# Loads of k and v in runs of 18 rows, and both modes of a pair in one 128-row product with a zero-padded block

## The chip, the core and the metric

The kernel runs on one core of one Trainium2 chip. A core has five engines that run side by side and wait for each other through semaphores: TensorE (PE, matrix products; PEld is its weight load), VectorE (DVE), ScalarE (ACT), GpSimd (POOL) and SyncE (SP). In this kernel POOL and SP mainly issue transfers, which 16 DMA engines carry out. POOL's transfers form one queue, served in order of issue; it also converts float32 to 16 bits on the way. SP's form another. The metric is the device time of one execution in microseconds (us), lower is better; the time given is the median of several executions.

## The reference

Two layers follow each other. With phi(x) = elu(x) + 1, the first is a linear attention over 8 batches, 8 heads, 576 rows and 64 columns:

```python
kv  = einsum('bhsd,bhse->bhde', phi(k), v)
z   = sum(phi(k), axis=2)
x   = einsum('bhsd,bhde->bhse', phi(q), kv) / (einsum('bhsd,bhd->bhs', phi(q), z) + 1e-6)
```

Its result is reordered to x of 8 x 576 x 512. The second is a spectral mix with a residual and a channel product:

```python
X = rfft(x, axis=1)                       # the first 64 modes are used
Yr[m] = Xr[m] @ w_r[m] - Xi[m] @ w_i[m]   # one 512x512 pair of matrices for each mode
Yi[m] = Xr[m] @ w_i[m] + Xi[m] @ w_r[m]
u = x + irfft(Y, n=576, axis=1)
out = u + relu(u @ w_ch)
```

The inputs are float32: q, k and v of 9.4 MB each, w_r and w_i of 67 MB each. The output is 9.4 MB of float32.

## The kernel before, in words

**Stage A, attention and forward transform.** `load(b)` has POOL fetch q, k and v of batch b (L179 to L194). q arrives in runs of 18 rows of a head (2304 bytes at 16 bits) and two such runs per partition; k and v arrive in runs of 9 rows (1152 bytes) and four per partition, one for each pair of heads. `exps` (ACT) and `features` (DVE) form phi; `features` also copies v into `vp`, beside a column of ones. `turn_q` transposes phi(q). `sum_kv` (L254) forms the products of phi(k) and v, with z as the 65th column: for two head groups and nine rows, two products of 64 partitions each, in the two halves of PE's rows. Two ACT copies bring the sums to `kv_all`. `form_x` divides and makes x. `transform` multiplies x by the Fourier matrix, and `place_x` spreads the result over partitions, into `xt_c` (DVE and ACT copies, L349 and L350). The raw tiles of q, k and v have two buffers each, so batch b + 2 is loaded when b is used up. Within a loop step the order on each engine is that of the program (`pin`).

**Mode products.** The weights come in pairs of modes: a tile `w` holds both modes of a pair, the first in partitions 0 to 63, the second in 64 to 127 (`w_load`, L114, one transfer for w_r and one for w_i, 1 MB each at 16 bits). Pairs 0 to 4 have buffers of their own and are queued during stage A. After them, in the same queue, stand `wch16` and `pick_sb`, a small table of ones and zeros. From pair 5 on there are two buffers, so POOL issues pair p + 2 when the products of p are done. `mode_pair` (L465) multiplies each pair: for 16 slices `dc`, one product of 64 rows for either mode (`product`, L435), into four 32-row strips of a PSUM tile for each mode, 32 products in all. `evacuate` copies the two PSUM tiles out, one on DVE (L452) and one on ACT (L454). `picks` (L457) sums the four strips with `pick_sb`, four products for each mode, into `yt_ps`, which a DVE copy takes out every fourth pair. Between the products and the picks, and after them, `work_slot` runs pieces of other work (attention rows again for the output, the inverse transform, the channel product), shared out over the pairs. `keep_warm` adds filler products in late pairs. The last pair has its own routine, `last_pair` (L488): its weights lie over all 128 partitions, and its last transfers are small pieces.

**Output.** When the last mode is known, 18 pairs of accumulators are finished one after the other: PE adds the rest of the inverse transform (L736) and `e0` (L775), ACT applies the relu, DVE adds x (L809), and SP stores (`store`, L787). One accumulator pair is 512 KB of output. `QUADS` (L802) names batches whose two halves are stored together once both are done, in runs of 8 KB; the others go half by half in runs of 4 KB. The tiles of rows 512 to 575 and the first few tiles go in runs of 2 KB.

Of the kernel before, what the change touches and what calls it, by code (L numbers as in the profile page):

```python
# [10 lines left out]
F32 = mybir.dt.float32  # L11
F16 = mybir.dt.float16
BF16 = mybir.dt.bfloat16
# [3 lines left out]
NJ = 9  # L17
# [3 lines left out]
def _dft_consts(S: int, NM: int):  # L21

    m = np.arange(NM)
    s_cols = np.concatenate([4 * np.arange(128) + jj for jj in range(4)] + [512 + np.arange(NP)])
    s_rows = np.concatenate([s_cols, s_cols[512:]]).reshape(5, 128).T
    ang = 2.0 * np.pi * s_rows[:, :, None] * m / S
    by_parity = np.concatenate([m[0::2], m[1::2]])
    fwd = np.concatenate([np.cos(ang)[:, :, by_parity], -np.sin(ang)[:, :, by_parity]], axis=2)

    scale = np.where(m == 0, 1.0, 2.0) / S  # L30
    ang = 2.0 * np.pi * np.outer(m, np.arange(S)) / S
    inv = np.empty((NM, 2, S), dtype=np.float64)
    inv[:, 0, :] = np.cos(ang) * scale[:, None]
    inv[:, 1, :] = -np.sin(ang) * scale[:, None]
    pick = np.zeros((128, 16), dtype=np.float16)
    for quad in range(4):
        for c in range(16):
            pick[quad * 32 + c, c] = 1.0

    return fwd.astype(np.float16), inv.reshape(2 * NM, S).astype(np.float16), pick  # L40
# [3 lines left out]
def kernel(  # L44
# [10 lines left out]
    nc = tc.nc  # L55

    B, H, S, Dh = q.shape
    D = H * Dh
    NM = moe_w_r.shape[0]
    NHP = H // 2  # L60
    NDC = D // 128
    NJJ = 4
    NDW = 4 * NDC
    NDL = NDW // 2
    NMP = NM // 2
    XDC = 2 * B * NMP
    NL = 8
    NE = NM - NL
    NF = NM // 2
# [10 lines left out]

    id16 = const.tile([128, 128], F16, name="id16")
    fwd_sb = const.tile([128, 5, 2 * NM], F16, name="fwd_sb")
    pick_sb = const.tile([128, 16], F16, name="pick_sb")
    wch16 = const.tile([128, NDC, D], F16, name="wch16")
    actwarm = const.tile([128, 1], F32, name="actwarm")
    nc.vector.memset(actwarm, 0.0)
# [4 lines left out]

    def xt_cols(dc: int, kk: int, n: int):

        if kk // 2 == LAST:
            part, dc = slice(0, 128), (dc // NDC * 2 + kk % 2) * NDC + dc % NDC
        else:
            part = HALVES[kk % 2]
        c0 = dc * XDC + kk // 2
        return xt_c[part, c0 : c0 + (n - 1) * NMP + 1 : NMP]


    QW = 4 * NJ * NP
# [5 lines left out]
    pin = tc.keep_in_program_order  # L108
# [31 lines left out]
    psA = psA_ctx.enter_context(tc.tile_pool(name="psA", bufs=1, space=bass.MemoryType.PSUM))  # L140
    n_pre, n_keep = W_PRE, W_KEEP

    vp = sA.tile([128, NHP, NJ, 66], F16, name="vpad")
    nc.vector.memset(vp[:, :, :, 64:66], 1.0)

    pending = [(p, half) for p in range(n_keep + n_pre) for half in range(2)]
# [31 lines left out]
    def load(b):  # L178
        for nm, src in (("q", q), ("k", k), ("v", v)):  # L179
            rows_in = src[b].rearrange("h s d -> (h s) d").rearrange(  # L180
                "(hp r j) d -> r hp (j d)", r=128, j=2 * NJ if nm == "q" else NJ
            )
            if (nm, b) == ("q", 0):
                for c in range(2):
                    t = sA.tile([128, 2, NJ * Dh], F32, tag="x16", bufs=2, name=f"q32_{c}")
                    pin(nc.sync.dma_start(out=t, in_=rows_in[:, :, c * NJ * Dh : (c + 1) * NJ * Dh]))
                    raw[nm, b, c] = t
                pin(nc.sync.dma_start(out=id16, in_=id16_dr.ap()))
                pin(nc.sync.dma_start(out=fwd_sb, in_=fwd_dr.ap()))
                continue  # L190
            shape = [128, 2, 2 * NJ * Dh] if nm == "q" else [128, NHP, NJ * Dh]
            t = sA.tile(shape, F16, tag=f"{nm}16", bufs=2, name=f"{nm}16_{b}")
            pin(nc.gpsimd.dma_start(out=t, in_=rows_in))
            raw[nm, b] = t  # L194

    def heads(nm, b, c):
        if (nm, b) == ("q", 0):
            return raw[nm, b, c].rearrange("p o (j d) -> p o j d", d=Dh)
        if nm == "q":
            return raw[nm, b].rearrange("p o (c j d) -> p c o j d", c=2, d=Dh)[:, c]  # L200
        return raw[nm, b].rearrange("p (o c) (j d) -> p c o j d", o=2, d=Dh)[:, c]

    def flat(nm, b):
        tiles = [raw[nm, b, c] for c in range(2)] if (nm, b) == ("q", 0) else [raw[nm, b]]
# [48 lines left out]

    def sum_kv(b):  # L254

        kv_ps = psA.tile([128, 2, 512], F32, tag="big", bufs=3, name=f"kvp{b}")
        for hpp in range(2):
            for j in range(NJ):
                for h2 in range(2):
                    pin(  # L260
                        nc.tensor.matmul(
                            kv_ps[:, h2, hpp * 130 : hpp * 130 + 130],
                            phi["k", b][HALVES[h2], hpp, j].rearrange("p o d -> p (o d)"),
                            vp[HALVES[h2], hpp::2, j, 0:65],
                            start=(j == 0),
                            stop=(j == NJ - 1),
                        )
                    )
        for hpo in range(2):
            rows = HALVES[hpo]  # L270
            pin(
                nc.scalar.copy(  # L272
                    out=kv_all[b][rows],
                    in_=kv_ps[rows, :, 0:260].rearrange("p t (c o n) -> p c t o n", c=2, o=2)[
                        :, :, :, hpo, :
                    ],
                )
            )

    def form_x(b, jj):  # L280
        if jj == 0:
# [150 lines left out]
            if work:  # L432
                work.pop(0)()

    def product(P, kk: int, w, dc: int):  # L435
        last = kk // 2 == LAST
        n_dc = NDL if last else NDW
        c = dc % NDC * 32
        n = 32 if dc < NDC else 2 * B
        rows = slice(0, 128) if last else HALVES[kk % 2]  # L440
        pin(
            nc.tensor.matmul(  # L442
                P[c : c + n, :], xt_cols(dc, kk, n), w[rows, dc, :],
                start=(dc < NDC), stop=(dc >= n_dc - NDC), tile_position=(rows.start, c),
                skip_group_check=True,
            )
        )

    def evacuate(kk: int, P):
        st = ystage.tile([128, D], F16, tag="ystage", bufs=2, name=f"ys{kk}")  # L450
        if kk % 2 == 0:
            pin(nc.vector.tensor_copy(out=st, in_=P))  # L452
        else:
            pin(nc.scalar.copy(out=st, in_=P))  # L454
        return st

    def picks(kk: int, st):  # L457
        for ec in range(NDC):
            pin(
                nc.tensor.matmul(  # L460
                    yt_ps[:, ec, kk % 8, :], st[:, ec * 128 : ec * 128 + 128], pick_sb
                )
            )

    def mode_pair(p: int):  # L465
        nonlocal yt_ps
        w = w_get(p)
        kks = (2 * p, 2 * p + 1)
        if p % 4 == 0:
            yt_ps = psW.tile([128, NDC, 8, 2 * B], F32, tag="yt", bufs=1, name=f"yt{p // 4}")  # L470
        Ps = [psW.tile([128, D], F32, tag="P", bufs=2, name=f"P{kk}") for kk in kks]
        for dc in range(NDW):
            for P, kk in zip(Ps, kks):
                product(P, kk, w, dc)
        sts = [evacuate(kk, P) for P, kk in zip(Ps, kks)]
        work_slot(p, "mid")
        for kk, st in zip(kks, sts):
            picks(kk, st)
        if p % 4 == 3:
            if kks[1] < NF:  # L480
                pin(nc.vector.tensor_copy(out=YE_T[:, :, kks[1] - 7 : kks[1] + 1, :], in_=yt_ps))
            else:
                g = (kks[1] - NF) // NL + 1
                pin(nc.vector.tensor_copy(out=YL[:, :, :, g, :], in_=mode_rows(yt_ps)))
        work_slot(p, "end")
        keep_warm(FILL.get(p, 0))

    def last_pair():  # L488
        w = w_get(LAST)
        kk = NM - 2  # L490
        work_slot(LAST, "start")
        P = psW.tile([128, D], F32, tag="P", bufs=2, name=f"P{kk}")
        for dc in range(NDL):
            product(P, kk, w, dc)
        st = evacuate(kk, P)
        work_slot(LAST, "mid")
        picks(kk, st)
        pin(nc.vector.tensor_copy(out=Y8[:, :, 0 : NL - 1, :], in_=yt_ps[:, :, 0 : NL - 1, :]))
        keep_warm(3)
        kk = NM - 1  # L500
        y_last = psW.tile([128, NDC, 2 * B], F32, tag="P", bufs=2, name="y_last")
        for dc in range(NDL):
            for ec in range(NDC):
                pin(
                    nc.tensor.matmul(
                        y_last[:, ec, :], w[:, NDL + dc, ec * 128 : ec * 128 + 128],
                        xt_cols(dc, kk, 2 * B),
                        start=(dc == 0 and ec == 0), stop=(dc == NDL - 1), skip_group_check=True,
                    )
                )  # L510
        nc.vector.tensor_copy(out=Y8[:, :, NL - 1, :], in_=y_last)
# [29 lines left out]

    yt_ps = None

    for p in range(n_early):
        mode_pair(p)
    wpre_ctx.close()
# [252 lines left out]
            in_=x_tail[i // 2],  # L799
        )  # L800

    QUADS = (2, 4, 5, 6)  # L802

    def finish(n: int):
        acc = accs[n]
# [190 lines left out]
```

## Time and profile before

| | us |
|---|---|
| median of 9 runs (lowest to highest) | 425.06 (424.51 to 426.32) |
| the profiled execution | 426.32 |
| its span, first to last instruction | 424.5 |
| PE busy (share of the span) | 278.5 (66%) |
| DVE busy | 215.0 (51%) |
| ACT busy | 161.0 (38%) |
| POOL busy | 56.7 (13%) |
| queue of POOL's transfers | 16512 packets, 81.47 MB |
| queue of SP's transfers | 3680 packets, 11.22 MB |

Mean granted PE clock: 0.788 of full. Busy shares are means over stages that have different limits. The page has six parts: busy time, the span in 40 slices with tenths of busy time and the DMA rate, the queues, the chain of work that ended last, the groups of instructions, and the transfers. A stretch of time in the profile gives a line with its length, the busy time and the number of instructions of PE, PEld, DVE, ACT and POOL, the granted PE clock, the share of the DMA engines' time that packets took (over 1 where they overlap) and the GB/s moved.

### The profile page before, as it was taken

To read this page: it belongs to the slowest core of one execution; us is meant where nothing else is said; L and a number is where in the kernel's file an instruction comes from. 1 tells how busy PE (TensorE), PEld (TensorE's weight loads), DVE (VectorE), ACT (ScalarE), POOL (GpSimd) and SP (SyncE) were. 2 spreads that over 40 slices of the span, in tenths; PEclk is the share of its full clock that TensorE was granted. 3 is DMA by queue.
4 is the path that set the end of the run, shared out by engine and by line. 5 is a ranking of instruction groups with operands and counts; after the bars stand their busy time and mean duration, and the time that the engine had idled before them with its cause. 6 is when DMAs were issued, how large, how long until landed. Compare 5 with 4: busy or idle time off the path is not lost.

```text
span 424.5 us, 7976 instructions
## 1 busy us (share of the span) xinstructions
PE 278.5 (66%) x3426; PEld 149.7 (35%) x3426; DVE 215.0 (51%) x446; ACT 161.0 (38%) x253; POOL 56.7 (13%) x99
## 2 busy tenths in 40 slices
PE   1358377688516644434344777989797698989991
PEld 0246266566302322212122232434343333455320
DVE  4599489895203453355444443445263323413892
ACT  4688487844202102000000243445354341421881
POOL 4222124210000100000000011100000000030000
PEclk9999888989755555555555598889899986998997
DMA  9999999999999999999999999999999999994697
GB/s 214 209 209 215 207 218 203 227 207 218 223 212 220 215 215 213 219 218 215 214 219 216 216 213 219 216 217 213 218 218 217 215 215 218 216 209 97 247 411 283
DMA packets 20227, 93.20 MB, mean 220 GB/s; under 512 B 2016, under 2 KB 11104, under 8 KB 15520
## 3 DMA queue, kind: packets, MB, share of 16 engines
q0 software_dynamic: 16512, 81.47, 93.6%
q1 hardware_dynamic: 3680, 11.22, 7.0%
q8 instruction: 27, 0.44, 0.4%
q14 instruction: 8, 0.07, 0.0%
HBM read 163.93 MB, written 9.44 MB: 408 GB/s over the span
## 4 chain that ended last, share of the span: by engine, by line
DMA 63%; PE 22%; DVE 5%; ACT 4%; issue 3%; POOL 2%; DVEq 0%; POOLq 0%; ACTq 0%
DMA w<-in_moe_w_i_dram 48%; PE P L442 8%; DMA pick_sb<-row_pick 8%; DMA k<-in_k_dram 7%; PE acc L736 3%; PE acc L775 2%; PE zl L425 2%; ACT ke L213 2%; POOL w L119 1%; PE eps L677 1%; ACT qT L249 1%; DVE ys L452 1%; PE z L699 1%; PE yt L460 1%; DVE x L299 1%
## 5 line engine op out<-in xcount | busy, mean ns | idle before, releaser
L442 PE MATMUL P<-w,xt_c 64*32 64x512 bf16 (+2 forms) x1000 | 51.7, 545 | 58.7 <-DMA w<-in_moe_w_i_dram 57.3
L452 DVE CAST ys<-P 128x512 f16<-128x512 f32 x32 | 22.1, 691 | 124.0 <-PE P L442 124.0
L454 ACT CAST ys<-P 128x512 f16<-128x512 f32 x31 | 18.1, 585 | 155.9 <-PE P L442 155.9
L119 POOL DMA_DIRECT2D w<-in_moe_w_r_dram x31 | 17.0, 550 | 245.9 <-PE P L442 96.4
L442 PEld LDWEIGHTS <-xt_c 64*32 64x32 bf16 (+2 forms) x1000 | 16.6, 128 | 79.3 <-DMA w<-in_moe_w_i_dram 46.1
L165 PEld LDWEIGHTS <-qT 64*128 64x128 f16 (+1 forms) x640 | 22.9, 123 | 51.6 <-issue 29.2
L677 PE MATMUL eps<-wch,xTw 128*128 128x512 f16 x144 | 40.8, 411 | 0.0
L165 PE MATMUL num<-kv,qT 64*128 64x65 f16 (+1 forms) x320 | 13.8, 211 | 27.3 <-ACT kv L272 13.8
L658 DVE TENSOR_TENSOR x_main<-ya,x_main 128x512 f32<-128x512 f32 x32 | 21.9, 688 | 15.0 <-PE ya L654 14.9
L660 ACT CAST x16w<-x_main 128x512 f16<-128x512 f32 x32 | 19.8, 618 | 23.5 <-DVE x_main L658 22.4
L165 PE MATMUL nw<-kv,qT 64*128 64x65 f16 (+1 forms) x320 | 19.0, 240 | 9.4 <-DVE x_tail L621 4.3
L685 ACT CAST E<-eps 128x512 f16<-128x512 f32 (+1 forms) x40 | 21.2, 540 | 9.2 <-PE eps L677 9.2
L460 PE MATMUL yt<-pick_sb,ys 128*128 128x16 f16 x252 | 11.7, 174 | 17.8 <-DMA pick_sb<-row_pick 11.2
L299 DVE TENSOR_TENSOR x<-num,rd 128x512 f16<-128x512 f32 x32 | 22.1, 691 | 1.1
L213 ACT ACTIVATE qe<-q 128x1152 f16<-128x1152 f16 (+1 forms) x16 | 17.9, 1157 | 11.0 <-DMA q<-in_q_dram 10.9
L242 PE MATMUL qTp<-id,qe 128*128 128x128 f16 x144 | 14.1, 276 | 10.1 <-DVE qe L226 9.5
L249 ACT COPY qT<-qTp 128x1152 f16<-128x1152 f16 x16 | 19.6, 1296 | 0.4 <-PE qTp L242 0.2
L460 PEld LDWEIGHTS <-ys 128*128 128x128 f16 x252 | 9.7, 102 | 28.4 <-DVE ys L452 15.0
L213 ACT ACTIVATE ke<-k 128x1152 f16<-128x1152 f16 x16 | 17.7, 1152 | 4.9 <-DMA k<-in_k_dram 4.9
L425 PE MATMUL zl<-wch,id 128*128 128x512 f16 x72 | 19.5, 406 | 0.0
L785 ACT ACTIVATE acc<-acc 128x512 f32<-128x512 f32 x34 | 18.1, 582 | 2.4 <-PE acc L736 1.2
L119 POOL DMA_DIRECT2D w<-in_moe_w_i_dram x31 | 16.9, 544 | 4.1 <-DMA q<-in_q_dram 2.3
(113 smaller groups left out, 460.3 us busy)
## 6 DMA issues: line engine op xcount, KB each, us to landing
w<-in_moe_w_r_dram POOLq DMA_DIRECT2D x31, 1024.0 KB, 12.2
w<-in_moe_w_i_dram POOLq DMA_DIRECT2D x31, 1024.0 KB, 16.9
k<-in_k_dram POOLq DMA_DIRECT2D x8, 576.0 KB, 12.8
v<-in_v_dram POOLq DMA_DIRECT2D x8, 576.0 KB, 14.9
out_dram<-x_main SPq DMA_DIRECT2D x4, 1024.0 KB, 4.9
q<-in_q_dram POOLq DMA_DIRECT2D x7, 576.0 KB, 12.9
out_dram<-x_main SPq DMA_DIRECT2D x6, 512.0 KB, 4.6
q<-in_q_dram SPq DMA_DIRECT2D x2, 576.0 KB, 4.5
```

Of the source, the lines that this page charges most:

```text
L119: nc.gpsimd.dma_start(out=w_in[p][half::2], in_=two.rearrange("g (r dc) e -> (g r) dc e", dc=NDW))
L165: mm = nc.tensor.matmul(num[hpo][orow, c0 : c0 + 65], qT[rows, hpp, h2, cols], kv_sb[rows, hpp, h2, :])
L213: pin(nc.scalar.activation(out=ev[:, c], in_=heads(nm, b, c), func=AF.Exp))
L249: nc.scalar.copy(out=qT[:, :, c * NJ : (c + 1) * NJ], in_=qT_ps.rearrange("p j x -> p x j"))
L299: nc.vector.tensor_tensor(out=dst.rearrange("p (o c d) -> p o c d", o=2, c=4), in0=nv[:, :, :, 0:64], in1=rden.unsqueeze(3).broadcast_to([ ...
L425: pin(nc.tensor.matmul(last_ps[0], id16, wch16[:, 0, :]))
L442: nc.tensor.matmul(P[c : c + n, :], xt_cols(dc, kk, n), w[rows, dc, :], start=(dc < NDC), stop=(dc >= n_dc - NDC), tile_position=(rows.sta ...
L452: pin(nc.vector.tensor_copy(out=st, in_=P))
L460: nc.tensor.matmul(yt_ps[:, ec, kk % 8, :], st[:, ec * 128 : ec * 128 + 128], pick_sb)
L658: pin(nc.vector.tensor_tensor(out=x, in0=acc, in1=x, op=ALU.add))
L677: nc.tensor.matmul(e_ps, xT[:, c, :], wch16[:, c, :], start=(c == 0), stop=(c == NDC - 1))
L685: pin(nc.scalar.copy(out=dst, in_=e_ps[:, cols]))
```

## The change

Four edits:

- k and v are loaded in runs of 18 rows like q. A partition then holds rows of two heads, and 32 partitions hold one head of each. So `sum_kv` works in 32-row groups: for each of two pairs of groups, 18 rows and two groups, 72 products for a batch in place of 36. Each pair has its own PSUM tile, and there are four ACT copies of 64x130 in place of two of 64x260.
- In `mode_pair` both modes multiply as one product over 128 partitions. The stationary block `xz` has 32 columns: 16 for the first mode, which are zero in partitions 64 to 127, and 16 for the second, which are zero in partitions 0 to 63. Two such blocks are cleared once; `set_diagonal` fills the next pair's with two DVE copies, ahead of `evacuate`. There are 16 products for a pair in place of 32, one PSUM tile, and one evacuation, on DVE for even and on ACT for odd pairs.
- `picks` handles both modes at once: `pick_sb` has 32 columns, and there are four products for a pair in place of eight.
- `QUADS` holds batches 5 and 6 only; batches 2 and 4 are stored half by half.

The last pair keeps its products.

```diff
-    pick = np.zeros((128, 16), dtype=np.float16)
+    pick = np.zeros((128, 32), dtype=np.float16)
...
-    vp = sA.tile([128, NHP, NJ, 66], F16, name="vpad")
+    vp = sA.tile([128, 2, 2 * NJ, 66], F16, name="vpad")
...
             rows_in = src[b].rearrange("h s d -> (h s) d").rearrange(
-                "(hp r j) d -> r hp (j d)", r=128, j=2 * NJ if nm == "q" else NJ
+                "(hp r j) d -> r hp (j d)", r=128, j=2 * NJ
             )
...
-        kv_ps = psA.tile([128, 2, 512], F32, tag="big", bufs=3, name=f"kvp{b}")
-        for hpp in range(2):
-            for j in range(NJ):
+        for pair in range(2):
+            kv_ps = psA.tile([128, 2, 512], F32, tag="big", bufs=3, name=f"kvp{b}_{pair}")
+            for j in range(2 * NJ):
                 for h2 in range(2):
+                    r0 = 64 * pair + 32 * h2
                     pin(
                         nc.tensor.matmul(
-                            kv_ps[:, h2, hpp * 130 : hpp * 130 + 130],
-                            phi["k", b][HALVES[h2], hpp, j].rearrange("p o d -> p (o d)"),
-                            vp[HALVES[h2], hpp::2, j, 0:65],
+                            kv_ps[:, h2, 0:130],
+                            phi["k", b][r0 : r0 + 32, j // NJ, j % NJ].rearrange("p o d -> p (o d)"),
+                            vp[r0 : r0 + 32, :, j, 0:65],
...
+                            tile_position=(r0, 0),
                         )
                     )
...
+            for hpo in range(2):
+                rows = HALVES[hpo]
+                pin(
+                    nc.scalar.copy(
+                        out=kv_all[b][rows, pair], in_=kv_ps[rows, :, hpo * 65 : hpo * 65 + 65]
+                    )
+                )
...
+    def set_diagonal(p: int):
+        for h in range(2):
+            src = xt_v[HALVES[h], :, :, :, p].rearrange("p c t b -> p c (t b)")
+            pin(nc.vector.tensor_copy(out=xz[p % 2][HALVES[h], :, h, :], in_=src))
...
-        Ps = [psW.tile([128, D], F32, tag="P", bufs=2, name=f"P{kk}") for kk in kks]
+        P = psW.tile([128, D], F32, tag="P", bufs=2, name=f"P{p}")
         for dc in range(NDW):
-            for P, kk in zip(Ps, kks):
-                product(P, kk, w, dc)
-        sts = [evacuate(kk, P) for P, kk in zip(Ps, kks)]
+            product(P, xz[p % 2][:, dc].rearrange("p h n -> p (h n)"), 32, w, dc, NDW)
+        if p + 1 < LAST:
+            set_diagonal(p + 1)
+        st = evacuate(p, P)
         work_slot(p, "mid")
-        for kk, st in zip(kks, sts):
-            picks(kk, st)
+        picks(2 * p, st, 2)
...
+    xz = [ystage.tile([128, NDW, 2, 2 * B], BF16, name=f"xz{i}") for i in range(2)]
+    for i in range(2):
+        nc.vector.memset(xz[i], 0.0)
+    set_diagonal(0)
     for p in range(n_early):
         mode_pair(p)
...
-    QUADS = (2, 4, 5, 6)
+    QUADS = (5, 6)
```

## The prediction

> **What bounds the kernel now.** I read the page's slices first, then its chain, then the transfer queues in short stretches, then the order of instructions at the end.
>
> ```profile
> DMA  9999999999999999999999999999999999994697
> GB/s 214 209 209 215 207 218 203 227 207 218 223 212 220 215 215 213 219 218 215 214 219 216 216 213 219 216 217 213 218 218 217 215 215 218 216 209 97 247 411 283
> ...
> DMA 63%; PE 22%; DVE 5%; ACT 4%; issue 3%; POOL 2%; DVEq 0%; POOLq 0%; ACTq 0%
> DMA w<-in_moe_w_i_dram 48%; PE P L442 8%; DMA pick_sb<-row_pick 8%; DMA k<-in_k_dram 7%; PE acc L736 3%; PE acc L775 2%; PE zl L425 2%; ACT ke L213 2%; POOL w L119 1%; PE eps L677 1%; ACT qT L249 1%; DVE ys L452 1%; PE z L699 1%; PE yt L460 1%; DVE x L299 1%
> ```
>
> The 16 DMA engines are full in 37 of 40 slices. Loads keep them full until about 386 us, then there is a hole of some 7 us around 390, then the stores run. In the chain, matrix products (PE P L442) are 8%; even those lie between landings of w. So up to 386 us the time is bytes over rate: work on PE, DVE and ACT counts there only if it lets the queue run empty. After that, it counts.
>
> The rate isn't the same everywhere. Stretches by time, with GB/s last; in each, the transfer counts tell what is in flight:
>
> ```profile
> 12.20:14.00 1.80, 0.00 (x0) 0.10 (x1) 1.76 (x3) 0.00 (x0) 0.00 (x0) 1.00 1.13 218
> 15.00:20.00 5.00, 2.09 (x36) 1.81 (x35) 2.19 (x3) 3.96 (x4) 1.29 (x2) 1.00 1.21 208
> 51.20:53.00 1.80, 0.52 (x10) 0.46 (x10) 0.06 (x1) 1.20 (x2) 0.00 (x0) 0.50 1.11 212
> 77.00:80.00 3.00, 1.67 (x43) 1.42 (x41) 2.97 (x5) 2.98 (x5) 0.54 (x1) 1.00 1.21 206
> 150.00:340.00 190.00, 122.08 (x1395) 56.12 (x1395) 84.61 (x217) 50.62 (x93) 20.08 (x38) 0.71 1.02 216
> ```
>
> The transfers of the second stretch alone:
>
> ```profile
> DMA packets 920, 1.04 MB, mean 208 GB/s; under 512 B 17, under 2 KB 920, under 8 KB 920
> ```
>
> Every packet is under 2 KB, so it is k and v. At 12.2 to 14 and 51.2 to 53 nearly all are above 2 KB: q. So k and v move at 206 to 209, q at 209 to 218, w at 216.
>
> At the end, stores and their gap (columns as above):
>
> ```profile
> 400.00:402.00 2.00, 2.00 (x14) 0.57 (x12) 2.00 (x3) 1.90 (x4) 0.00 (x0) 1.00 0.99 401
> 402.00:404.00 2.00, 2.00 (x16) 0.57 (x12) 1.92 (x3) 1.68 (x4) 0.00 (x0) 1.00 0.51 209
> 410.00:417.00 7.00, 5.29 (x32) 1.50 (x30) 6.92 (x6) 4.78 (x10) 0.00 (x0) 1.00 1.00 411
> ```
>
> And 402 to 404 in 40 slices of 0.05 us:
>
> ```profile
> DMA  9979959200000000000000000009993009999003
> ```
>
> 19 empty slices, from 402.40 to 403.35: for 0.95 us there is nothing to send, while DVE is at work.
>
> **What the Trainium skill says.** "DMA: Bandwidth & Descriptors", section "Why small descriptors are slow (HBM only)": each packet pays a fixed few cycles and each transfer fixed metadata, so longer runs are faster. The trace agrees in sign (208 against about 213). "Perfetto Trace Analysis", section "DMA Optimizations": runs under 2 KB are costly and batching up to 8 KB can help a lot. Here the help is small: stores in 4 KB runs make 401, in 8 KB runs 411. "TensorE: Matmul & The Clock Gate", section "Part 3: Packing small matmuls — row/col tiling": products in different row or column groups overlap. The trace agrees: 32 products of 64x512 take 1.10 us at full clock, not 32 times 0.2.
>
> **The change part by part.**
>
> *Loads.* 16 loads of 576 KB, 9.44 MB, go from 1152-byte to 2304-byte runs, as q has. 9.44/207.5 is 45.5 us, 9.44/212.5 is 44.4: 1.1 us less; I take 1.0. If q's rate in a short stretch is chance and equals k's, 0; if q reached w's 216, 1.8.
>
> *k-v sums (stage A).* 36 products per batch become 72, still two row groups at once, since a pair's products are all issued before the other's. 36 took 1.22 to 1.45 us, so PE gets 1.2 to 1.5 more; if 32-row products don't overlap, up to 3.7. ACT copies: two of 64x260 at 0.37 become four of 64x130, about 0.30 each by the slope between 256 columns (0.39) and 512 (0.585): 0.45 more. Behind the second pair's copies on ACT stand the next exps; `num` on PE waits for them, and DVE for that; the v copy to `vp` waits for the last product, and v's next load for the copy. I take a slip of 1.2 us a batch, off the path: q of batch 7, the closest load, is issued at 67.84 and lands 9.2 later, of which its own bytes take 2.8 and, as an estimate, 2 are fixed: over 4 us of cover, against one sum between the landing that feeds it (49.5) and it. Pair 5's w is issued at 114.81, after stage A, and its first half lands 15.6 later: less 4.9 and 2, 8.7 us of cover against five sums, 6 us. Also the first picks wait for pick_sb until 125.65 (issued at 92.73, 32.92 to landing, by the chain in order of time) while their input is ready at 115.3. So it costs 0.
>
> *Products.* 32 of 64x512 become 16 of 128x512. The last pair's 8 of that shape take 0.66 us; twice that, less one start, is about 1.1: equal to the 1.10 of 32. At half clock both are four rounds, 1.95. Evacuations halve (0.69 on DVE or 0.58 on ACT, in turn, before on both at once); picks fall from 8 (0.36) to 4 (0.26), twice as wide. Added: two `set_diagonal` copies a pair, 64 partitions by 256 elements. No row has this shape; 128x64 takes 0.20 and an elementwise 128x256 0.42: 0.3 each, bounds 0.2 and 0.45, so 0.6 us of DVE a pair, less 0.35 for the evacuation saved every other pair. They stand ahead of `evacuate` on DVE, and run while PE works or waits on w. DVE is busy 84.61 of 190 us there. Two memsets (0.27) and the first copies delay pair 0 by 1.2 us, under the wait for pick_sb. Without that cover it would be 1.2. Once: pair 30 to the last product is PE without idle, from w's landing at 380.71 to 391.6; its picks and fewer weight loads save 0.2 us there.
>
> *Stores.* b = 2 and b = 4 go in two halves. DVE finishes an accumulator pair every 1.22 us from 397.67; b=2's first half is ready at 401.3 and can flow at 402.4, when DMA falls idle, in place of 403.35. From there to 421.5 DMA is full, so 0.95 us comes off the end, less 2.1 MB at 401 in place of 411 (0.13) and a new gap of about 0.15 before b=5's 1 MB: 0.7. It can't exceed 3.6: the last store (512 KB), issued at 417.05, lands 6.5 later; the 1 MB one that was issued into the empty queue took 4.2, so half of it with nothing ahead would take about 2.9.
>
> *Sum.* On the profiled execution, 426.32 (span 424.5 and 1.8 around it): 1.0 + 0.2 + 0.7 = 1.9 less, 424.4. That run is the slowest of nine; their median is 425.06, so 423.2, 0.45% faster.
>
> **The rivals.**
>
> 1. *The gains are taken back (no change).* The loads' gain is as small as 0.3, because 208 against 213 is read from stretches of 2 us; or the store gap only moves, as a 1 MB store still waits for both halves of b=5. For it: the spread of q's stretches. Against it: all four k-v stretches lie within 206 to 209. One gain missing leaves 0.3 to 0.9 us: 424.5.
>
> 2. *The 32-row products run one after another and the queue runs dry (slower).* Two now share 68 ns; alone, 72 take 4.9 us, 3.7 more a batch. Five such slips, about 17 us after overlap, exceed the 8.7 of cover at pair 5's w: the queue stands empty 8 to 9 us near 126. Net 425.06 + 8.5 - 1.9 = 431.7. It decides from 1.7 us a batch. Against it: today's two groups do overlap.
>
> 3. *DVE becomes late for products (less gain).* If `set_diagonal` took over 1 us and stood behind the folds, PE would wait for it, not for w. Cover: w is issued with 6 us of other transfers ahead. It would need 6 us a pair; it could only show at pair 30, some 0.5 to 1 us: 424.0.
>
> **How the numbers follow.** Both gains, rival 3 with them: 0.64, 422.3 to 424.2, likeliest 423.2. Rival 1: 0.20, 424.2 to 425.9. Rival 2: 0.08; slower by what I don't see: 0.08. The range, 422.3 to 425.8, leaves out the slower cases and a little on either side. A difference under 0.2% (0.85 us) can't be told from none: faster 0.66, same 0.18, slower 0.16.
>
> **What would show it.** Loads right: k-v stretches at 211 to 215 GB/s, and pick_sb landing at about 124.7 in place of 125.65. Stage A right: products of pair 0 before 121, DMA slices still 9 throughout. Products right: L442's successor about 1.1 us a pair at full clock. Stores right: no empty DMA at 402, end 1.5 to 2 us earlier. I am wrong if a slice near 115 to 130 or 140 shows DMA below 9, or if PE is at half clock when the stores begin: a half-rate PE couldn't feed them.

## The result, and the profile after

The changed kernel takes 422.03 us (median of 10 runs, 421.43 to 424.69); the kernel before, run beside it, 425.74 (32 runs). The ratio is 0.9926, 95% interval 0.9913 to 0.994: 0.74% or 3.15 us faster (2.6 to 3.7). The prediction said 1.9 us, 423.2. The direction holds, but the gain is 1.25 us larger, and the time lies 0.3 below the low end of the range (422.3). That margin is thin: timed again (below) the same kernel took 422.35, just inside the range. The record also lists two runs, 422.58 and 424.09, that are not among the ten; with them the median would be 422.33.

The times of either kernel fall into groups 1 to 1.5 us apart (of the changed one, a profiled execution with PE at half clock after the last weights took 423.18, one without it 421.84), so times are compared below by ratios with their intervals, and places in the trace by their own records.

The profiled execution after is 423.18 us (span 421.4), against 426.32 (424.5): 3.14 less. Its slices, its transfers and its chain, the lines that answer to those shown of before:

```profile
PEclk9999998589855555555555598899799896899897
DMA  8999999999999999999999999999999999996797
GB/s 217 211 212 216 210 219 207 225 221 207 222 214 222 220 205 222 219 205 223 219 210 218 219 215 213 219 217 213 220 216 210 221 221 207 221 210 128 245 392 311
DMA packets 16417, 93.17 MB, mean 221 GB/s; under 512 B 2032, under 2 KB 2944, under 8 KB 11968
...
q8 instruction: 24, 0.39, 0.3%
...
DMA 63%; PE 22%; DVE 5%; issue 3%; ACT 3%; POOL 2%; DVEq 0%; ACTq 0%; POOLq 0%
```

DMA stays at 9 from the second slice to the hole near 388: the loads set the time up to there, as before. The hole is shallower (6 and 7 in place of 4 and 6). There are 8160 fewer packets under 2 KB than the 11104 of before. The line to keep in mind is the least conspicuous: queue q8 carries *instructions* (packets, MB, share of the DMA engines' time). Before it read:

```profile
q8 instruction: 27, 0.44, 0.4%
```

Three packets fewer, of 16 KB each. That is 0.05 MB of 93, and, as is shown below, it is where most of the unforeseen gain comes from.

The new groups of instructions (line, engine, operation, tiles; then busy us and mean ns of one; then idle time before them):

```profile
L431 PE MATMUL P<-w,xz 128*32 128x512 bf16 x496 | 47.6, 523 | 64.2 <-DMA w<-in_moe_w_i_dram 61.8
...
L256 PE MATMUL kvp<-vpad,ke 32*128 32x130 f16 x576 | 24.3, 261 | 8.9 <-ACT qT L243 6.1
L441 DVE COPY xz<-xt_c 64x256 bf16<-64x256 bf16 x62 | 23.0, 371 | 11.0 <-PE P L431 10.1
```

Products wait for w as before. `set_diagonal` takes 371 ns a copy (0.3 estimated), the k-v products 24.3 us of PE in all (11.8 before).

Stretches after (length, busy us and number of PE, PEld, DVE, ACT, POOL, then PE clock, DMA share, GB/s). The first three hold k and v, the last two the end of the loads and the first stores:

```profile
15.00:20.00 5.00, 2.05 (x36) 1.77 (x36) 2.19 (x3) 4.06 (x4) 1.16 (x2) 1.00 1.11 213
24.00:28.00 4.00, 1.85 (x38) 1.28 (x38) 3.72 (x15) 2.56 (x5) 1.44 (x2) 1.00 1.11 213
75.00:78.00 3.00, 3.00 (x62) 2.81 (x61) 1.43 (x2) 2.39 (x4) 0.54 (x1) 0.50 1.11 211
384.00:392.00 8.00, 7.57 (x68) 3.79 (x67) 2.52 (x5) 1.12 (x3) 0.45 (x1) 0.80 0.25 45
392.00:400.00 8.00, 8.00 (x42) 3.05 (x40) 6.80 (x8) 6.83 (x13) 0.12 (x1) 0.98 0.88 307
```

And the last two stretches before:

```profile
384.00:392.00 8.00, 7.68 (x84) 3.63 (x80) 1.96 (x4) 0.59 (x1) 0.00 (x0) 0.96 0.42 79
392.00:400.00 8.00, 7.75 (x43) 3.73 (x44) 5.84 (x8) 6.04 (x13) 0.57 (x1) 1.00 0.63 209
```

k and v move at 211 to 213 (206 to 209 before). From 392 to 400 DMA is busy 88% in place of 63%: the stores begin earlier.

Where the 3.14 us come from is seen in the chain of waits in order of time (start, length, what), at its two turns. Before:

```profile
362.95 17.72 DMA w<-in_moe_w_i_dram
380.71 1.55 PE P L442 x24
...
390.71 0.92 PE y_last L505 x32
```

After:

```profile
91.74 33.08 DMA pick_sb<-row_pick
125.13 1.86 PE P L431 x12
...
362.71 25.30 DMA w<-in_moe_w_i_dram x2
388.67 0.47 PE ypl L908 x4
```

`pick_sb` lands at 124.82 (125.65 before). Then, near 362.8, the second half of pair 30's w is issued at nearly the same time in both, and waits in a full queue. Before it took 17.72 us to land; after, the list of transfers issued there has

```profile
w<-in_moe_w_i_dram POOLq DMA_DIRECT2D x1, 1024.0 KB, 15.4
```

which is 2.3 less, though the first of its 16 engines was only 1.0 us earlier (374.42 against 375.43). Second, before, PE was the last at the end: the last piece of w landed at 389.89, but `y_last` was done only at 391.65. After, the last piece lands at 388.02 and `y_last` is done at 388.39, right behind it; the chain runs through transfers there ("x2"), and PE waits for them.

The timeline at that point after (start, duration, engine, instructions, in brackets the idle time before and who ended it):

```profile
388.39 0.22 DVE L508 CAST Y<-y_last 128x64 f16<-128x64 f32 x1 [1.58 <-PE y_last L502]
388.67 0.47 PE L908 MATMUL ypl<-id,Y 128*128 128x128 f16 x4 [0.32 <-DVE Y L508]
...
392.82 2.94 SPq L792 DMA_DIRECT2D out_dram<-x_main  x4
```

From the end of `y_last` to the first store 4.43 us pass, before 3.33 (391.65 to 394.98). The difference is PE's clock: half of full for one stretch of 3.41 us. The kernel before has such a stretch too, but earlier, at the products of pair 30. The two stretches, before and after (columns as above):

```profile
381.22:384.63 3.41, 3.41 (x41) 1.41 (x26) 1.08 (x2) 0.58 (x1) 0.00 (x0) 0.50 1.02 210
388.86:392.27 3.41, 3.38 (x16) 1.84 (x14) 1.15 (x3) 1.12 (x3) 0.57 (x1) 0.50 0.00 0
```

So the difference of the two profiled executions divides like this: last piece of w 1.87 earlier, of which 1.0 is the load stream itself and 0.85 the slowest DMA engine; PE no longer late behind it, 1.4; PE at half clock before the first store, 1.1 back; from the first store's issue to the end 28.6 in place of 29.5, 0.95. Together 1.0 + 0.85 + 1.4 - 1.1 + 0.95 = 3.1. The 1.4 and the 1.1 both go with the half clock (for the first, see the kernel with the instructions put back), so they belong to these two executions as much as to the kernels, and nearly cancel.

### The profile page after: what moved, and what is told of

Same layout as the page of the kernel before. It is cut to its first block, busy times and chain, and to the rows that moved or that the text cites. A ratio compares the mean times of both kernels' runs of the same rounds, so it can differ in the third digit from the quotient of the medians.

```text
span 421.4 us, 7345 instructions
## 1 busy us (share of the span) xinstructions
PE 291.4 (69%) x3094; PEld 157.2 (37%) x3094; DVE 228.1 (54%) x495; ACT 154.0 (37%) x253; POOL 57.0 (14%) x99
## 2 busy tenths in 40 slices
DMA packets 16417, 93.17 MB, mean 221 GB/s; under 512 B 2032, under 2 KB 2944, under 8 KB 11968
## 4 chain that ended last, share of the span: by engine, by line
DMA 63%; PE 22%; DVE 5%; issue 3%; ACT 3%; POOL 2%; DVEq 0%; ACTq 0%; POOLq 0%
DMA w<-in_moe_w_i_dram 51%; DMA pick_sb<-row_pick 8%; PE P L431 7%; DMA k<-in_k_dram 3%; PE acc L737 3%; PE kvp L256 2%; PE acc L776 2%; POOL w L116 2%; DVE x L292 1%; PE eps L678 1%; PE zl L418 1%; ACT ke L207 1%; PE ya L655 1%; PE xTp L668 1%; ACT qT L243 1%
## 5 line engine op out<-in xcount | busy, mean ns | idle before, releaser
L431 PE MATMUL P<-w,xz 128*32 128x512 bf16 x496 | 47.6, 523 | 64.2 <-DMA w<-in_moe_w_i_dram 61.8
L448 ACT CAST ys<-P 128x512 f16<-128x512 f32 x15 | 8.8, 585 | 130.8 <-PE P L431 130.8
L431 PEld LDWEIGHTS <-xz 128*32 128x32 bf16 x496 | 13.3, 115 | 85.4 <-DMA w<-in_moe_w_i_dram 53.6
L446 DVE CAST ys<-P 128x512 f16<-128x512 f32 x17 | 11.8, 691 | 50.9 <-PE P L431 50.9
L256 PE MATMUL kvp<-vpad,ke 32*128 32x130 f16 x576 | 24.3, 261 | 8.9 <-ACT qT L243 6.1
L441 DVE COPY xz<-xt_c 64x256 bf16<-64x256 bf16 x62 | 23.0, 371 | 11.0 <-PE P L431 10.1
L256 PEld LDWEIGHTS <-ke 32*128 32x128 f16 x576 | 22.2, 115 | 10.7 <-issue 8.4
L622 DVE TENSOR_TENSOR x_main<-nw,rd 128x256 f32<-128x256 f32 x32 | 11.2, 414 | 17.3 <-PE nw L162 17.3
L670 DVE COPY xTw<-xTp 128x512 f16<-128x512 f16 x36 | 15.0, 416 | 9.3 <-PE xTp L668 9.3
L454 PE MATMUL yt<-pick_sb,ys 128*128 128x32 f16 (+1 forms) x128 | 8.9, 187 | 15.7 <-DMA pick_sb<-row_pick 9.5
## 6 DMA issues: line engine op xcount, KB each, us to landing
w<-in_moe_w_r_dram POOLq DMA_DIRECT2D x31, 1024.0 KB, 12.8
```

Of the source, the lines that this page charges most:

```text
L256: nc.tensor.matmul(kv_ps[:, h2, 0:130], phi["k", b][r0 : r0 + 32, j // NJ, j % NJ].rearrange("p o d -> p (o d)"), vp[r0 : r0 + 32, :, j, 0 ...
L431: nc.tensor.matmul(P[c : c + n, :], x, w[:, dc, :], start=(dc < NDC), stop=(dc >= n_dc - NDC), tile_position=(0, c), skip_group_check=True,)
L441: pin(nc.vector.tensor_copy(out=xz[p % 2][HALVES[h], :, h, :], in_=src))
```

## What the slowest DMA engine carries

A transfer of w is split over 16 DMA engines, and PE waits for the last of them. The trace has the 16 landings of each transfer. For pair 30's second half, in us after the first of them (rounded; two of the kernels are introduced below):

```
before                       0.0 0.3 0.3 0.5 0.8 0.8 1.4 2.1 | 3.1 3.3 3.5 3.5 3.5 3.7 3.7 5.2
after                        0.0 0.1 0.2 0.2 0.5 0.6 0.6 2.3 | 2.4 2.4 3.3 3.5 3.5 3.5 3.7 3.7
products alone               0.0 0.0 0.1 0.1 0.3 0.4 0.8 2.1 | 2.1 2.2 2.3 2.5 3.4 3.5 3.5 3.6
products, instructions back  0.0 0.1 0.2 0.3 0.3 0.5 1.0 2.1 | 3.4 3.4 3.4 3.4 3.5 3.5 3.6 4.8
```

Seven engines keep up (left of the bar). The eight right of it lag by steps of 1.1 to 1.2 us: two, three, and in two kernels one engine by four. One more, the last left of the bar, lags by 2.1 to 2.3 in all of them; why was not looked into. At the start, all 16 land within about 0.5 us. The last landing jumps right after the 1st, 9th, 17th and 25th packet of q8: before, those packets pass at 29.9, 116.3, 248.9 and 378.6 us, and the last landing jumps at 33.2, 118.3, 252.7 and 380.7. The same four jumps, as far as there are that many packets ahead of the last weights, stand in all 13 traces. One such packet keeps its DMA engine 0.89 to 0.98 us.

This fits packets that go round eight of the 16 engines, so that every eighth puts the same engine further behind; while the queue is full, the engine doesn't make that up. The trace doesn't name a packet's engine, but the packets' own durations say the same. Before, the first eight take 935, 975, 974, 961, 893, 893, 948 and 944 ns, and the next eight repeat these to within 15 ns, as do the eight after them. Every trace has this cycle of eight, entered at different places, with a few single packets that take longer. The numbers fit too: ahead of pair 30's landing 25 packets have passed before (three for seven engines, four for one), 22 after (three for six, two for two) and 20 with the products alone (three for four, two for four); these are the groups of lags right of the bar.

What are these packets? The Trainium skill, "Runtime: NRT & Kernel Launch", section "Instruction fetch mechanics", says that an engine's sequencer refills its instructions over a DMA queue of its own, in blocks of 16 KiB, 256 instructions. The trace agrees in number: PE has 6852 instructions before (3426 products, 3426 weight loads), and 6852/256 is 26.8, with 27 packets; after, 6188 give 24.2, with 24 packets. The page calls the cost mostly hidden. For PE the runs here show nothing against that; for the DMA engine that carries the packet, in a kernel whose DMA is always full, it isn't hidden.

The **fetch theory** is then: the change saves PE 664 instructions, so the 25th fetch, which fell at 378.6, ahead of the last pieces of w, isn't there before they land. The rival is the **path theory**: the gain comes from PE having fewer and shorter steps at the end. The table has all kernels that were run; each ratio is to runs of the kernel before made beside it (medians of 425.66 to 425.79).

| kernel | PE instructions | fetches; when the 25th | last piece of w landed | median, us | ratio to before (95%) |
|---|---|---|---|---|---|
| before | 6852 | 27; 378.6 | 389.89 | 425.74 | 1 |
| after, again | 6188 | 24; none | 387.97 | 422.35 | 0.993 (0.9911 to 0.995) |
| after, 816 more for PE | 7004 | 27; 368.1 | 389.08 | 422.49 | 0.9939 (0.9922 to 0.9957) |
| after, 384 more for PE | 6572 | 25; 388.8 | 387.79 | 421.86 | 0.9918 (0.9903 to 0.9933) |
| after, PE's time alone | 6260 | 24; none | 388.00 | 422.42 | 0.9932 (0.9908 to 0.9956) |
| loads alone | 7428 | 29; 343.4 | 389.12 | 423.76 | 0.9969 (0.9958 to 0.9981) |
| products alone | 5612 | 22; none | 388.88 | 423.61 | 0.9962 (0.9949 to 0.9975) |
| stores alone | 6852 | 27; 378.4 | 389.73 | 425.22 | 0.9987 (0.9978 to 0.9997) |
| after, warm end | 6198 | 24; none | 387.80 | 422.04 | 0.9937 (0.992 to 0.9954) |
| products alone, instructions back | 6860 | 27; 375.0 | 389.92 | 425.12 | 0.999 (0.9982 to 0.9998) |
| after, stores undone | 6188 | 24; none | 388.11 | 422.77 | 0.9928 (0.9912 to 0.9944) |
| after, all in halves | 6188 | 24; none | 387.84 | 422.09 | 0.9928 (0.9907 to 0.9949) |

## The experiments

### More instructions for PE in the kernel after

The kernel after, unchanged, gives the level:

> The changed kernel, unaltered, for comparison on the same chip: 422.0 us, about 3.7 less than before.

Measured: 422.35, ratio 0.993. The level stands.

Then tiny products, whose results nothing reads, are added at the ends of pairs 6 to 17, long before the end:

```diff
+        if 6 <= p < 18:
+            for _ in range(34):
+                pin(nc.tensor.matmul(last_ps[0][:, 0:16], id16, wch16[:, 0, 0:16]))
```

> The changed kernel with 408 tiny extra matrix products (816 instructions of TensorE with their weight loads), in pairs 6 to 17 where TensorE waits for weights; their results are never read. Theory F (fetches): TensorE's own instructions arrive as 16 KB transfers, each holds up one of the 16 DMA engines for 0.95 us, and every eighth meets the same engine, which then lands last; with 816 more, the fetch with number 24 comes back before the last weights, so pair 30's weights and the last piece land about 1 us later and the time rises by 1 us, to 423.0. Theory P (TensorE's path): the extra gain came from shorter products behind the last weights; pairs 6 to 17 wait for weights anyway, so nothing changes: 422.0. Both: 27 fetches or more in the queue of instructions in place of 24.

The same with 16 in place of 34:

> The same with 192 tiny products (384 instructions). Theory F: one or two fetches more, but number 24 still comes after the last weights: no change, 422.0. If every fetch costs its share of all 16 engines (0.95/16 us) instead, +0.1. Theory P: 422.0.

(These two texts count the fetches from 0: their number 24 is the 25th of the table.) And PE's time without the instructions: three products of 512 columns in place of the 34 of 16:

> The same TensorE time in few instructions: 36 products of 512 columns (72 instructions) in pairs 6 to 17. Theory F: the number of fetches stays 24: 422.0. If busy time on TensorE and not the number of instructions is what costs, as much as with 816 instructions: 423.0.

Measured, in the order of the table: the 25th fetch comes at 368.1 with 816 more, and the last piece of w lands 1.1 us later (389.08 against 387.97). The chain of that kernel:

```profile
373.11 14.71 DMA w<-in_moe_w_i_dram
...
387.96 1.13 PE y_last L505 x28
389.09 0.04 issue
389.13 0.30 PE y_last L505 x4
```

The last four products of `y_last` wait for that piece. With 384 more the 25th fetch comes at 388.8, after the last weights, and nothing is later (387.79). PE's time with few instructions delays nothing (388.00); it is 13.7 us more of busy PE, where the 816 instructions make 18.4. This is what the fetch theory says of *landings*: it isn't instructions as such, but whether the 25th comes in time to delay the weights. In the *time* the intervals don't tell the three apart: 0.9939, 0.9918 and 0.9932 against 0.993. The 423.0 that the fetch theory expected with 816 more did not come (422.49); that its fastest run took 422.35, where the fastest of the other three took 421.32 to 421.66, points its way. As a test of the time this was too weak; a stronger one follows below.

### The edits one at a time

The kernel before with only the loads in runs of 18 rows and the k-v sums that go with them:

```diff
-                "(hp r j) d -> r hp (j d)", r=128, j=2 * NJ if nm == "q" else NJ
+                "(hp r j) d -> r hp (j d)", r=128, j=2 * NJ
```

> The kernel before with the k and v loads and their sums of the change alone. Theory L (load rate): 1.0 us less, 424.7 where before is 425.7; k and v then move at 212 to 213 GB/s in place of 208. TensorE has 576 instructions more, so about two fetches more (29), but still four of them on the slowest engine before the last weights: theory F adds nothing. If the k-v sums slow the loads: 426 or more.

With only the products, the picks and their copies:

```diff
-        for dc in range(NDW):
-            for P, kk in zip(Ps, kks):
-                product(P, kk, w, dc)
+        for dc in range(NDW):
+            product(P, xz[p % 2][:, dc].rearrange("p h n -> p (h n)"), 32, w, dc, NDW)
+        if p + 1 < LAST:
+            set_diagonal(p + 1)
```

> The kernel before with the one-product pairs, the block and the wide picks alone. TensorE has 1240 instructions fewer: about 22 fetches in place of 27, and three on the slowest engine before the last weights in place of four. Theory F: the last piece lands 0.95 us earlier, and 1.0 to 1.5 us are gained in all. The prediction's own step: 0.2. If set_diagonal is in the way: 0 or slower.

With only the stores:

```diff
-    QUADS = (2, 4, 5, 6)
+    QUADS = (5, 6)
```

> The kernel before with the stores of batches 2 and 4 in halves alone. The prediction's step: 0.7 us less, and no empty DMA at 402. From the two traces: 0.4, since part of the gap shows up elsewhere.

Measured, by ratio: loads 0.31% (1.3 us, 0.8 to 1.8), products 0.38% (1.6 us, 1.1 to 2.2), stores 0.13% (0.55 us, 0.1 to 0.9). They add up to 3.45, the whole is 3.15: within their intervals the edits add up. Loads and stores are near the 1.0 and 0.7 predicted; the products are eight times the 0.2 predicted. Their chain at pair 30:

```profile
362.01 17.00 DMA w<-in_moe_w_i_dram
379.01 0.04 issue
379.05 1.05 PE P L435 x16
...
388.93 0.30 PE y_last L506 x4
```

The loads are those of before here, and the first engine is done with this w at the same time (375.36, before 375.43); the last is done 1.7 us earlier (379.01 against 380.67). With 22 fetches there is no 25th. And `y_last` ends in four products that wait for the last piece: PE isn't late.

The loads alone, by contrast, make PE's instructions more (288 more products in the k-v sums, 29 fetches, the 25th at 343.4), and the last piece still lands 0.8 earlier (389.12): the 25th came in time before too, and a 33rd isn't reached.

### The products alone, with PE's instructions put back

The kernel with the products alone, and 52 tiny products a pair (624, each with its weight load, so 1248 instructions), which bring PE to 6860 instructions, as before:

```diff
+        if 6 <= p < 18:
+            for _ in range(52):
+                pin(nc.tensor.matmul(last_ps[0][:, 0:16], id16, wch16[:, 0, 0:16]))
```

> Of the edits only the products (both modes as one product, with the picks and copies that go with it), and the 624 instructions of PE that this edit saved are put back as tiny products of 16 columns, 52 a pair in pairs 6 to 17, whose results nothing reads; PE then has as many instructions as in the kernel before. Fetch theory (the edit gains because PE's instructions, fetched by DMA, are fewer): the gain falls to 0.2 to 0.4 us, 425.3 to 425.5, with 29 or so fetches and the last piece of w landing about 1 us later than with the products alone (888.9 there is read as 388.88). Path theory (the edit gains because PE has fewer and shorter steps after the last weights): nothing changes, 423.6. Both in part: half way, 424.5.

Measured: 425.12, ratio 0.999 (0.9982 to 0.9998), 0.4 us faster than before; the kernel with the products alone was 1.6. The intervals don't meet. Three quarters of the gain are gone, with nothing changed but PE's instructions in pairs 6 to 17, more than 100 us before the end, and the time that these take on PE (12.8 us more busy). And it isn't the median alone: the fastest of the 20 runs (424.62) is slower than eight of the nine with the products alone (up to 423.81). The chain:

```profile
361.91 18.17 DMA w<-in_moe_w_i_dram
380.08 0.04 issue
380.13 1.90 PE P L435 x13
...
389.94 0.92 PE y_last L509 x32
```

Pair 30's w is issued at the same time as without them (361.91, 362.01), and its first engine is done at the same time (375.28, 375.36); the last is 1.1 us later (380.08, 379.01). The last piece lands at 389.92, as before (389.89). The path theory said 423.6; the shorter path is all there, and most of the gain is not. It falls. What busy time on PE costs by itself was tried only in the kernel after (above), where it moved no landing.

Whether PE is late at the end is another matter, and the fetches alone don't decide it. Here PE, which had waited 2.2 us for pair 30's w, multiplies it at half clock (1.90 in place of 1.05), and has no idle time up to the end of `y_last`. In four of the 13 traces `y_last` ends 0.9 to 2.0 us after the last piece of w; in the others 0.3 (0.7 in one that is told below). The four are just those with a stretch of half clock between 366 and 386 us: the kernel before, the stores alone (382.20 to 385.62), this one (380.01 to 383.42), and the kernel after with its stores undone (366.11 to 372.94). The last of these has no 25th fetch. The other way round, the loads alone and the kernel after with 816 more do have one in time, and PE isn't late. In the first three PE had been idle for 1.7 to 2.1 of the 3.41 us just before, waiting for w. A late fetch lengthens this wait and may so bring the half clock on; that is not shown.

### Is the half clock at the end a loss that can be taken back?

In the profiled execution after, PE ran at half clock from 388.86 to 392.27. The Trainium skill, "TensorE: Matmul & The Clock Gate", section "Part 1: The HAM clock gate (the "warmup" mystery)", says that the clock is granted by how busy PE was in a window of some 3.4 us, which runs freely, so that the same kernel falls into it differently from run to run. The trace agrees: one stretch of 3.41 us at 0.50 in one execution of the kernel after, none there in another (1.00 in "after, again"). More filler products ahead of `y_last` should keep PE busy:

```diff
-        keep_warm(3)
+        keep_warm(8)
```

> The changed kernel with eight filler products in place of three ahead of the last products (y_last), where TensorE waits for the last piece. Theory C (clock): the half clock from 388.6 to 392 is set off by the idle time just before; with the fillers it stays away, and the 1.1 us that the stretch from the last product to the first store took longer come back: 421.0 to 421.5. If the half clock has another reason, or if the fillers end after the last piece has landed: 422.0 to 422.5.

Measured: 422.04, ratio 0.9937: no gain over the kernel after. In its profiled execution PE is at full clock there, and from the end of `y_last` to the first store 3.33 us pass in place of 4.43; but so they do in "after, again", which has no fillers more. The fillers end late, too: `y_last` is done 0.7 us after the last piece, not 0.3. And the record doesn't show that idle time set the half clock off, for in the profiled execution after, PE was busy for 3.01 of the 3.41 us just before it. Of 14 runs, 11 lie from 421.75 to 422.19, where the kernel after spreads to 423.2; but three lie at 424.25 to 425.45 (two of 16 above 424 for the kernel after), and the medians are equal. None of the three was the profiled one, so what they have in common is open.

### The stores, undone and carried on

In the kernel after, batches 2 and 4 are stored whole again (`QUADS = (2, 4, 5, 6)`):

> The kernel after with the batches 2, 4, 5 and 6 stored whole, as before; everything else as changed. If the stores' share is what it was alone (0.55 us), 422.6 with the time of the kernel after at 422.0 to 422.4; if it overlaps with the others' gain because the stores now begin with PE at half clock, 422.2 or no difference. A gap of DMA of 0.5 to 1 us should stand again near 400.

And the other way, no batch is stored whole (`QUADS = ()`):

> The kernel after with no batch stored whole: batches 5 and 6 too go in halves of 4 KB runs. The gap of 0.23 us that stands ahead of the 1 MB store of batch 5 should close, against 0.1 us for runs of 4 KB in place of 8 KB on 2.1 MB: 0.1 us less to 0.1 us more than the kernel after, 422.0 to 422.4. If the last store's own latency counts, halves make it shorter and the gain is up to 0.3 us.

Measured: 422.77 (0.9928) undone, 422.09 (0.9928) with halves throughout, and the kernel after 422.03 and 422.35: no difference that these few runs can tell. The traces do tell the gaps apart. DMA in 40 slices each, in the kernel after from 396 to 400 (0.1 us a slice):

```profile
DMA  9899999999975443009999999999998879989999
```

In "after, again", from 394 to 402 (0.2 us a slice):

```profile
DMA  9999999999959999899999999899999999998989
```

With the stores undone, from 396 to 404 (0.2 us a slice):

```profile
DMA  9999999998599999989989992000099895993959
```

With halves throughout, from 395 to 415 (0.5 us a slice):

```profile
DMA  9989999999999998999999999999999999999999
```

Undone, the gap of about 1 us stands again, at 400.8 to 401.8. In the kernel after it is gone, but there is a dip at 397.2 to 397.8. That is an execution with half clock just ahead of the first store; "after, again", at full clock there, has no empty slice. With halves throughout DMA is full to the end, at 398 GB/s in this stretch; before, with 8 KB runs, it was 411 from 410 to 417. That 4 KB runs, being slower, take back what the closed gap gives fits these numbers, but 0.1 us can't be shown by them. No kernel of these is clearly better than the changed one.

## Why the prediction was right and wrong

**Loads: right.** It said 1.0 us. k and v move at 211 to 213, as named; packets under 2 KB fell from 11104 to 2944; `pick_sb` lands 0.83 earlier and the first engine of pair 30's second half 1.0 earlier. Alone, 1.3 (0.8 to 1.8).

**k-v sums: right.** It said 1.2 to 1.5 us more on PE for a batch, hidden. At full clock 72 products take 2.07 to 2.37 us where 36 took 1.22 to 1.45, about 0.9 more and so less than said; at half clock 3.64 where 36 took 2.13, 1.5 more. The two row groups do overlap, so rival 2 (from 1.7 a batch) had no ground. The products of pair 0 begin at 113.44, 0.9 later than the 112.52 of before and well before 121, and DMA stays at 9. What the step left out is that 288 more products are also two more fetches. (The 2 us of fixed time in its sums for the cover are an estimate that this trace bears out roughly: the 1 MB store into the empty queue took 4.2 us, its bytes at 411 GB/s about 2.6.)

**Products: the step that failed.** It said 0.2 us, only at the end, for picks and weight loads saved there. PE's figures were right: 1.05 us for 16 products (1.1 said), 1.90 at half clock (1.95 said), `set_diagonal` at 0.37 (0.3 said) and hidden. Measured alone, the step is worth 1.6. The prediction counted PE's instructions only as PE's time; they are also transfers, on the engines that bound the kernel, and for these its sum has nothing. It also took "PE without idle" from 380.71 to 391.6 for a property of the kernel; it goes with the half clock from 381.22 on, and the loads alone, with the old products, have no such lateness. Each pair drops 16 products and 4 picks, with as many weight loads, which makes 1240 instructions in 31 pairs: five fetches of 16 KB, one of which fell on the engine that was last. The last piece of w lands 1.0 us earlier for it. With the instructions put back it lands 1.04 later again and 0.4 us of the gain is left (0.1 to 0.8), not far from the 0.2.

**Stores: right.** It said 0.7; alone, 0.55 (0.1 to 0.9). The gap at 402 closed as said; the dip at 397 stands in the execution with half clock ahead of the stores and not in the one without.

**The sum.** 1.9 said, 3.15 measured. The products' error alone, 1.4, is about the whole difference of 1.25. The two medians of before (425.06 of 9 runs, 425.74 of 32) differ by 0.7 as well, so the forecast stood on a low median. It is the difference of 1.9 that was wrong; how little the time missed the range is owed to chance as well.

**Rival 1** fell with the loads' and stores' gains both there; **rival 3** showed nowhere. The sign that was to prove the prediction wrong, PE at half clock when the stores begin, nearly appeared: the half clock ends at 392.27, the first store is issued at 392.82. It cost 1.1 us in that execution, and the gain was larger in spite of it. As a danger it was rightly named, but not as a sign: it comes in some runs only.

## What to carry to other kernels

Where DMA is the bound, count the instruction fetches: PE's instructions (with their weight loads) over 256 is the number of 16 KB packets, they go, as far as the landings and their durations tell here, round eight of the 16 DMA engines, and the engine that has one more sets when every split transfer lands. The gain comes in steps (here, whether a 25th fetch comes before the last weights), so a saving may be worth 1 us or nothing. And when an edit gains more than its working says, put back one by-product of it at a time, here the bare number of instructions, before believing a story about its purpose. And before reading a wait or a lateness as a kernel's own, look whether the clock in that one execution made it.

## What was unexpected of the hardware

- One packet of instructions keeps one DMA engine for 0.89 to 0.98 us, in a cycle of eight durations, and the lag isn't made up while the queue is full: the 16 landings of a transfer, within about 0.5 us at the start, lie 5.2 us apart after 25 fetches (before), 3.7 apart after 22 (after).
- 384 more instructions for PE delayed the last weights by nothing, 816 by 1.1 us.
- Whether PE is late at the end goes with a stretch or two of 3.41 us at half clock: `y_last` is done 0.9 to 2.0 us after the last piece of w in the four traces that have one between 366 and 386 us, 0.3 to 0.7 in the other nine.
